# First batch's half loads in two 64-partition transfers of 1,024-byte runs, and unread products from a zeroed tile

## The chip, the cores and the metric

One core of a Trainium2 chip runs the kernel. TensorE (PE) multiplies matrices, VectorE (DVE), ScalarE (ACT) and GpSimd (POOL) work on tiles, and SyncE (SP) issues most of the DMA transfers. Each engine takes its instructions in the order of the program and waits on semaphores for the others. The metric is the device time of one execution in microseconds.

## The reference

Eight batches of causal attention with eight heads of 64 columns, 576 queries, and 592 keys (16 beacon keys that every query sees, then 576 causal ones); the result, as 4,608 rows of 512 columns, goes through a gated feed-forward layer.

```
k_all = np.concatenate([beacon_k, k], axis=2)
v_all = np.concatenate([beacon_v, v], axis=2)
scores = scale * np.matmul(q, k_all.transpose(0, 1, 3, 2))
scores = np.where(causal, -1000000000.0, scores)
a = softmax(scores)
x = (a @ v_all).transpose(0, 2, 1, 3).reshape(B * S, H * D)
out = (np.maximum(x @ w_gate, 0.0) * (x @ w_val)) @ w_out
```

Inputs and output are float32; the kernel multiplies in bfloat16.

## The kernel before

The whole work is cut into some 2,400 tasks. Each names its engine or engines, what it depends on and which tiles it holds, and a text constant `ORDER` in the source lists all of them in the order in which they are emitted, with the numbers of the buffers taken and, where a task may run on either of two engines, a letter (a ScalarE, v VectorE, g GpSimd). `replay` walks through this list, so each engine's program order is that of the list; a planner wrote it beforehand and is not part of the kernel. An entry such as `f12:7` stands for twelve unread products ("fills", line 1064): TensorE multiplies into bank 7, from which nobody reads, and so is kept at work while it would wait. Before the change a fill multiplies `ident` (a bf16 identity) with the zero part of `mask`. GpSimd makes both at the start (lines 436 to 444).

The first batch comes in halves. `load_half` (line 649 holds its transfer) loads 256 rows of four heads of q or k as a 128 x 512 float32 tile `st`, one transfer of 256 KB: each partition has two rows of each of four heads, so four runs of 512 bytes. There are eight such loads (k and q, two groups of four heads, two halves), all issued by SP. `rounded` (line 542) makes the bf16 tile `h`, on VectorE or GpSimd for this batch, and puts the columns of two heads side by side; `turned` (line 553) multiplies by `ident` to transpose it; an eviction (line 493 on ScalarE, 495 on VectorE) spreads the result into `kT` or `qT`. `load_rest` (line 677) does the same for the last 64 key rows with the 16 beacon rows, and for the first 64 and last 16 query rows, in runs of 256 bytes. Batches 1 and up load pairs of heads instead (line 587, runs of 1,024 bytes).

Scores (line 824) need halves and rest. For each block VectorE adds the mask and takes the minimum (line 772; q was negated), ScalarE takes the exponential with its sum (line 779), VectorE the reciprocal (line 785), GpSimd the product (line 790). For the first batch TensorE transposes the probabilities (line 900), for the others a DMA does (line 910, `pTb<-pb`, `pTa<-pa`). Line 920 and, for the last 16 queries of each head, 943 multiply by V. The feed-forward part (lines 981, 986 and 1012) runs over ten spans of 240 to 512 rows, each as soon as its rows are there; GpSimd issues the loads of the weights (line 507). Staging tiles `st` are eight buffers, taken in turn; a load waits until its buffer is free. Small memsets on VectorE zero the paddings of `qT` (469, 470), of `pa` and `pb` (463) and of the part of `xT` that holds the first batch's probabilities (485).

Of the kernel before, what the change touches and what calls it, by code (L numbers as in the profile page):

```python
# [10 lines left out]
BF16 = mybir.dt.bfloat16  # L11
# [66 lines left out]
10 1 22:0 2 26:1 34:3 0 4 30:2 23v:0.0 8 38:4 24:0 9 5 f4:7 42:5 27g:1.0 7 25v 48:7 28:1 46:6 35v:0 31v:2 36:3 29v 32:2 50:0 f3:7 37v 33a 54:1 f2:7  # L78
39v:1 410:4.5.0.0 58:2 11 431:6.0 6 40:1 411 43g:2 12 412 41a 423 44:2 413 45a 49g:0 422 3 436 414 448:3.1.0.0 62:7 415 421 f12:7 432 47g 426 68:5 450
416 459 70:6 449 425 460 51g:0 451 469:2.4 424 66:4 f1:7 417 437 461 14 52:5 427 433 55v:1 470 53a 418 56:6 434 f8:7 474 428 463 419 57v 471 429 462  # L80
420 59v:2 486:5.6.0.1 475 430 472 63v:0 454 473 438 487 64:2 453 435 60:7 464 69v 439 491 452 440:4 61a 72:0 476 495:3.1 13 73 441v:0 492 f3:7 455 465
496 488 444:0 467 f2:7 16 65v 504:4.5 497 77:1 489 500 442:2 445a:0 458 f3:7 505 457 f1:7 501 466 513:6.0 493 456 509 446:3 506 477 f1:7 f3:7 502 498
468 514 447a 443a 15 478:3 510 71v 482:4 518 522:1.2 515 19 511 524 479a:0 523:5.6 67g 516 519 483v:0 480:3 512 528 484:4 481a 18 525 548:7.3.2.3 485v
529 549 90:5 494 557:1.2 91 1734:4 553 17 550 1738:0 562 1735:0 566:5.6 507 503 1739:1 f2:7 558 563 1736:4 508 567 1742:7 559 490 1737:0 554 526 520
499 1740:4 571 1743:2 575:1.0 81:3 568 517 1741:1 82 1744:2 576 86:4 572 584:3.4 527 f1:7 580 1746:5 577 521 532:7 569 530 560 586 1747:1 531 536:1
533a:0 1748:5 1745:2 534:6 74:1.1 1749:3 537a 540:2 564 535v 587 78:2.1 95:0 544:5 542:1 541v:1 125:7 538:6 581 570 588 573 585:2.3 551 565 543a 555
539v 1750:0 561 545v 610:6.7.0 590 1751:1 552 546:4 589 578 611 591 1754:0 579 75:5 612 1752:1 1755:0 582 592 547v 76a 1756:3 574 613 1758:2 1757:5
593 594:4 1753:4 1759:0 596:5 556 595v:2 598:1 1762:0 583 614 79:7 597v 1760:4 1763:1 615 599a 602:2 1761:6 80a 606:5 87:1 616:1 604:4 617v:0 83:0
600:3 603v:3 92:2 101:3 84:6 601a 88:7 113:4 605v 607a 93:0 96:0 618:3 105:1 85a 89v 20 109:2 608:2 94a 99:6 97:5 126:1.0 609v 1766:1 98a 1764:4 619a
127:6 620:0.2.0.1 102:2 1765:7 128a 635:3.5 1770:7 1767:2 621 21 643 103:6 628 1768:4 622 1771:0 106:0 104a 1772:1 1769:8 624 1774:7 114:2 1773:9  # L90
1778:4 629 623 123:4 1776:1 1775:1 644 1779:2 1780:6 121:5 110:1 631 1792:4 1777:10 133:1 636 630 650:7.0 137:2 1781:11 1793:0 1787:2 637 129:0 645
646 659 107:6 652 639 111:4 1782:1 632 625 638 647 651 649 108a 112v 115:3 1788 633 653 640 116v 627 654 665:6.5 658 626 674:3.4 634 661 666 1794:7
642 660 670 1783 667 100:1 655 676 671 657 1784 119:6 124 677 700:0.6.2.3 1795:12 1785a:0 122 141:4 1796:5 701 679 117:3 668 656 708 715:7.1 702 678
648 1789 134:1 709 1797:1 704 669 717 145:1 1800:4 176:5 662 1790a:1 1798:3 716 664 723 703 1802:5 663 718 1799:13 641 1801:2 1804:2 724 1786 120 711
675:3.4 672 705 680 1803:14 149:6 1805:0 681 1806:0 726 683 682 1808:2 719 1807:15 673 690:3 1812:5 710 1809:1 712 130:0.0 730:6.0 684 725 1810:7 720
732 686 713 1814:1 738 1813:2 721 731 685 714 1816:5 1811:8 118 131:2 739 734 1818:4 687 1815:1 1817:1 689 745:3.7 733 1819:2 1820:1 688 741 735 746
754:5.6 132a 736 695:1 740 1822:4 750 722 1821:1 1824:0 757 142:0 747 1823:11 1828:1 151:7 707 751 756 755:3.4 138:2 1825:2 727 1832:2 742 748 758 737
# [12 lines left out]
913 961 1893:4 898 209a 220:2 973 211:2 960 1899:0 965 1894:1 955 964 962 1897:3 974 956:0 1896:1 1900:2 963 1901:6 1898:2 967 230:5 941:0 975 943:4  # L110
978 922 976 923 1903:1 977 214:7 944a 1902:3 227:1.0 942a 945:3 1904 966 979 221:1 980 986:5.3.4.6 225 1908:7 987 988 1913:0 215:0 998 991 981 968 201
1909 997 990 989 219 222:4 1910 999 242:1 992 256:6 957:5 1001 212:2 1911a:0 1905 213v 231:2.0 958a 1912 1000 216:5 970 238:2 1002 1906v:2 1914 234:7
993 217v 223 1007:3.4.6.7 946:1 995 250:4 1015 948:2 972 1918:5 949a 971 1016 252:3 985 1009 1915 1017 1907 947v 982 284:5 1008 983 1018 1105:1.2.1
268:0 228:6 1916a:1 1919 1106 1010 1917 1019 235:0 1107 1920 1011 229v 969 246:7 1108 1003 239:1 1923:3 1921v:0 1004 1109 1032:4.0.7.1.2.3 1110 1924:0
1925:2 1034 994 1111:1 996 1931:5 1033 1046 1038 1926:4 251:0 232:6 1927:3 1047 1932:2 264:4 1037 1012 1048 1013 1050 1929:2 1036 1051 1021 236:4 1035
1928:1 1933:5 233v 243:2 1039 1049 1040 1014 272:1 244:7 240:3 1930:5 247:0 237a 1022:0 1935:6 1053 245v 253:1 1112:4 1052 241v 1020 1936:0 1939:0
1934:6 1005 248:2 1113v 257:2 1059:1.5.3.7 249a 254:6 1940:1 1061 1943:4 255a 1070 260:6 1060 1937:2 1041 1944:2 1071 1043 1062 1947:6 1074 984 1054
1063 1938:3 1055 1941:0 1073 1006 1072 1064 1045 1945:2 1027:1 1065 273 1948:0 1949:1 1066 1044 1946:9 1075 269 1942:8 1080:3.4.5.6 1068 1025:2 1082
1058 1950:10 1023:0 1951:7 1026a 1057 1076 1042 1088 265:1 1955:1 1952:1 1081 1056 274:4 1957:2 1024v 1069 1922 1956:2 1089 1083 258:7 261:0 1953:0
1958:12 1090 1067 270:6 1078 1959:3 276:7 1091 1954:11 1079 1084 1092 262:1 259v 266:0 1093 1960:0 1114:5.4.2.6.0.1 286:3 263a 1028:7 275 1115 267a  # L120
1030:3 1128 1085 1077 1116 1029a 1961:1 1094 1031a 1129 1119 1087 1100:3 1967:7 1118 271 1132 1133 1962:13 1963:0 1120 1117 277:1.1 1130 1260:2.3.0
1131 1964:1 1965:5 1086 1968:0 1261 1135 278:1 1969:0 1966:14 1122 1095:2 1262 1971:7 1121 1263 1976:4 1134 1264 279v 1265 1141:5.3.6.2 1970:15 1977
1142 1123 1152 1972 1143 1266:0 1145 1144 1973 1146 1153 280:6 1147 1978 1974v:0 1155 1154 1981:3 1156 1975 1148 1979a:1 293:1 1162:0.1.5.6 1157 1980
# [199 lines left out]
def kernel(  # L323
# [12 lines left out]
    nc = tc.nc  # L336
# [181 lines left out]
    class Batch:  # L518
        pass

    batches = []

    def new_batch(b, prio, work):
        t = Batch()
# [573 lines left out]
```

## Time and profile before

| | us |
|---|---|
| median of two runs | 399.56 (399.12 to 400.01) |
| profiled execution, whole | 399.52 |
| its span on the core | 397.6 |

| engine | busy us | share of the span |
|---|---|---|
| PE | 380.1 | 96% |
| DVE | 274.2 | 69% |
| ACT | 270.3 | 68% |
| POOL | 231.0 | 58% |

A row of the timeline reads: start, duration, engine, line, operation, tile written and tile read, shapes, count, and in brackets the idle time before it with what ended it. SPq and ACTq are the queues in which these engines issue transfers. PEld is TensorE loading stationary tiles, beside its products. Matrix products are pipelined and their ends are modelled, so spacing says more than the duration of one.

### The profile page before, as it was taken

How to read it: one execution, taken by the hardware profiler on the slowest of the kernel's cores; microseconds unless marked ns; L12 is line 12 of the kernel's file. 1: busy time of each engine (PE TensorE's matmuls, PEld its weight loads, DVE VectorE, ACT ScalarE, POOL GpSimd, SP SyncE). 2: the span in 40 equal slices, each digit the busy share in tenths (PEclk: the TensorE clock that was granted, in tenths of full speed). 3: DMA queues.
4: the chain of work that ended last, by engine and by line, in shares of the span. 5: the costliest groups of instructions: out<-in, count | busy, mean ns of one | idle time of the engine just before them, and what ended most of it. 6: DMA issues, size and time to landing. Idle time of an engine off the chain costs nothing.

```text
span 397.6 us, 10026 instructions
## 1 busy us (share of the span) xinstructions
PE 380.1 (96%) x3384; PEld 199.7 (50%) x3428; DVE 274.2 (69%) x1008; ACT 270.3 (68%) x842; POOL 231.0 (58%) x447
## 2 busy tenths in 40 slices
PE   5789999999999999999999899999999999999996
PEld 3557855655454455454444454445444445444453
DVE  5899799888976888877876778567946832331230
ACT  1899699897877687789777789688746731332322
POOL 3799779959785789268827787663853650000000
PEclk9999999999999999999999999999999999999999
DMA  7999999999999999968997999988897556001102
GB/s 183 218 181 237 193 230 235 195 230 236 215 234 205 313 177 203 181 186 177 202 205 215 197 202 198 209 162 167 169 180 161 101 105 168 28 0 54 54 26 94
DMA packets 184100, 68.89 MB, mean 173 GB/s; under 512 B 158384, under 2 KB 179504, under 8 KB 184048
## 3 DMA queue, kind: packets, MB, share of 16 engines
q1 hardware_dynamic: 179216, 63.46, 74.5%
q0 software_dynamic: 4752, 4.72, 7.3%
q8 instruction: 27, 0.44, 0.5%
q14 instruction: 25, 0.20, 0.1%
q10 hardware_dynamic: 80, 0.07, 0.1%
HBM read 38.54 MB, written 9.44 MB: 121 GB/s over the span
## 4 chain that ended last, share of the span: by engine, by line
PE 83%; DMA 3%; issue 1%; DVE 1%; POOL 0%; ACT 0%; DVEq 0%
PE f L1012 22%; PE f L986 22%; PE f L981 22%; PE f L824 6%; PE f L920 6%; PE f L553 2%; DMA pTb<-pb 2%; DMA pTa<-pa 2%; PE f L943 1%; PE f L626 1%; PE f L874 1%; DVE f L772 0%; PE f L900 0%; POOL pa L790 0%; DVE kT L495 0%
## 5 line engine op out<-in xcount | busy, mean ns | idle before, releaser
L790 POOL TENSOR_SCALAR pb<-pb,small 128x384 bf16<-128x384 bf16 (+8 forms) x272 | 142.1, 538 | 45.5 <-DVE small L785 43.9
L779 ACT ACTIVATE pb<-f,small 128x448 bf16<-128x448 f32 (+8 forms) x272 | 144.8, 551 | 24.5 <-DVE small L772 19.7
L772 DVE CUSTOM_DVE_ANT_0 f<-f,mask 128x64 f32<-128x64 f32 (+8 forms) x288 | 136.3, 507 | 20.1 <-PE f L824 11.0
L997 DVE TENSOR_TENSOR hT<-g,f 128x512 bf16<-128x512 f32 (+3 forms) x120 | 74.4, 629 | 55.3 <-PE f L986 30.2
L981 PE MATMUL f<-xT,wg_r 128*128 128x512 bf16 (+3 forms) x466 | 108.1, 357 | 0.9 <-issue 0.2
L986 PE MATMUL f<-xT,wv_r 128*128 128x512 bf16 (+3 forms) x465 | 106.8, 357 | 1.2 <-issue 0.3
L1012 PE MATMUL f<-wo_r,hT 128*128 128x512 bf16 (+3 forms) x441 | 100.3, 374 | 1.5 <-issue 1.0
L992 ACT ACTIVATE g<-f 128x512 f32<-128x512 f32 (+3 forms) x120 | 65.8, 563 | 49.3 <-PE f L981 31.0
L981 PEld LDWEIGHTS <-wg_r 128*128 128x128 bf16 x480 | 45.0, 98 | 45.2 <-issue 2.5
L986 PEld LDWEIGHTS <-wv_r 128*128 128x128 bf16 x480 | 44.5, 98 | 44.2 <-issue 3.0
L1012 PEld LDWEIGHTS <-hT 128*128 128x128 bf16 (+3 forms) x456 | 41.9, 100 | 47.0 <-issue 2.9
L779 ACT ACTIVATION_READ_ACCUMULATOR pb<-f,small 128x1 f32 x272 | 60.0, 221 | 0.0
L542 POOL TENSOR_SCALAR h<-st 128x512 bf16<-128x512 f32 (+1 forms) x87 | 46.8, 547 | 22.5 <-DMA st<-in_q_dram 5.0
L772 DVE DVE_READ_ACCUMULATOR2_ANT small<- 128x1 f32 x296 | 41.2, 139 | 0.1
L824 PE MATMUL f<-kT,qT 64*64 64x64 bf16 (+7 forms) x640 | 34.6, 296 | 1.6 <-ACT pb L779 0.7
L497 POOL TENSOR_SCALAR v<-st 128x512 bf16<-128x512 f32 (+1 forms) x38 | 23.3, 616 | 19.7 <-DMA st<-in_v_dram 19.6
L493 ACT CAST xT<-f 128x240 bf16<-128x240 f32 (+2 forms) x46 | 16.1, 376 | 22.6 <-PE f L920 22.5
L785 DVE RECIPROCAL small<-small 128x2 f32<-128x2 f32 (+3 forms) x136 | 19.7, 160 | 12.0 <-ACT pb L779 10.8
L920 PE MATMUL f<-pTb,v 128*64 128x320 bf16 (+3 forms) x488 | 27.0, 254 | 0.4 <-DMA pTb<-pb 0.4
L824 PEld LDWEIGHTS <-qT 64*64 64x64 bf16 x640 | 14.7, 107 | 22.6 <-issue 17.7
L920 PEld LDWEIGHTS <-v 128*64 128x64 bf16 (+1 forms) x512 | 21.0, 109 | 9.9 <-issue 5.1
L553 PE MATMUL f<-ident,h 128*128 128x128 bf16 (+1 forms) x224 | 19.8, 222 | 5.7 <-DVE h L542 5.0
(62 smaller groups left out, 216.1 us busy)
## 6 DMA issues: line engine op xcount, KB each, us to landing
out_dram<-osb SPq DMA_DIRECT2D x34, 256.0 KB, 2.7
st<-in_k_dram SPq DMA_DIRECT2D x28, 256.0 KB, 4.6
st<-in_q_dram SPq DMA_DIRECT2D x28, 256.0 KB, 4.0
st<-in_v_dram SPq DMA_DIRECT2D x24, 256.0 KB, 4.6
st<-in_q_dram SPq DMA_DIRECT2D x16, 128.0 KB, 3.8
st<-in_k_dram SPq DMA_DIRECT2D x16, 128.0 KB, 4.1
st<-in_v_dram SPq DMA_DIRECT2D x8, 224.0 KB, 4.5
wv_r<-in_moe_w_val_dram POOLq DMA_DIRECT2D x3, 512.0 KB, 9.2
```

The costliest lines, as they stand in the source:

```text
L542: (nc.gpsimd if x.engine == "POOL" else nc.vector).tensor_scalar(to, src, by, 1.0, ALU.mult, ALU.mult)
L553: nc.tensor.matmul(to, h16.tile[:rows, a * P:(a + 1) * P], ident[:rows, :rows], start=True, stop=True)
L772: nc.vector.tensor_tensor_reduce(out=view(i, n - m), in0=view(i, n - m), in1=msk, scale=1.0, scalar=at(7) if m < n else 3.0e38, op0=ALU.ad ...
L779: nc.scalar.activation(ph.tile.rearrange("p a n -> p (a n)")[:, a:a + n], view(i), AF.Exp, bias=at(i), scale=-1.0, accum_out=at(4 + i))
L790: nc.gpsimd.tensor_scalar(one, one, at(8 + i), 1.0, ALU.mult, ALU.mult)
L824: nc.tensor.matmul(banks[k][b_].tile[64 * i:64 * i + 64, off:off + n], t.q.tile[r, 2 * g + i, 64 * j:64 * j + 64], t.kT.tile[r, 2 * g + i, ...
L920: nc.tensor.matmul(ps.tile[64 * hh:64 * hh + 64, d0:d0 + w], t.v.tile[:rows, c, D * h:D * h + D], rhs(64 * hh), start=(c == 0), stop=(c == ...
L981: nc.tensor.matmul(psg.tile[:, :mt], wg_r[:, ki, nf * P:(nf + 1) * P], xT[:, ki, m0:m0 + mt], start=(ki == 0), stop=(ki == KM - 1))
L986: nc.tensor.matmul(psv.tile[:, :mt], wv_r[:, ki, nf * P:(nf + 1) * P], xT[:, ki, m0:m0 + mt], start=(ki == 0), stop=(ki == KM - 1))
L992: r = add("ACT", c_act(mt), lambda _, psg=psg, g=g: nc.scalar.activation(g.tile[:, :mt], psg.tile[:, :mt], AF.Relu), (a,), (psg, g), -1000 ...
L997: hid.append(add("DVE", c_dve(mt), lambda _, psv=psv, g=g, nf=nf: nc.vector.tensor_mul(hT[nf].tile[:, :mt], g.tile[:, :mt], psv.tile[:, :m ...
L1012: nc.tensor.matmul(ps[c].tile[64 * c:64 * c + rows, :w], hT[nf].tile[:, t0:t0 + rows], wo_r[:, nf, w * c:w * c + w], start=(nf == 0), stop ...
```

## The change

- `load_half` issues two transfers for each load. Transfer i fills partitions 64 i to 64 i + 63 with the heads 4 g + i and 4 g + i + 2; each partition has four rows of two heads, so two runs of 1,024 bytes. The rounding depends on both. The shapes of rounding and eviction stay, their strides follow the new layout.
- Either transfer can go through SP's or ScalarE's queue. The order gives ScalarE the second halves of the first four loads, ahead of its table load; both halves of the last four loads are issued by SP, one after the other.
- A new tile `idle` is zeroed by VectorE, as its first instruction. The fills multiply it with itself, and no longer read `ident` and `mask`.
- `ORDER` is written anew, for the whole kernel, with nine tasks more. It has 53 fills and not 46; fourteen of them stand before the first transposition. GpSimd makes the causal helper of the last queries first, then `ident`, then `mask`. The first `qT` eviction goes to ScalarE.

```
+    idle = cp.tile([P, 256], BF16, name="idle")
...
+    def make_idle(_):
+        nc.vector.memset(idle, 0.0)
...
-            def fetch(_):
-                nc.sync.dma_start(st.tile.rearrange("p (h e) -> p h e", h=4),
-                                  src[b, 4 * g:4 * g + 4, s0:s0 + 256, :].rearrange("h (p j) d -> p h (j d)", j=2))
-
-            ld = add("DMA", (0.5, 0.95), fetch, (held,), (st,), prio[0])
+            st.users += 1
+
+            def fetch(i):
+                def run(x):
+                    (nc.scalar if x.engine == "ACT" else nc.sync).dma_start(
+                        st.tile[64 * i:64 * i + 64].rearrange("p (k e) -> p k e", k=2),
+                        src[b, bass.ds(4 * g + i, 2, step=2), s0:s0 + 256, :].rearrange("k (p j) d -> p k (j d)", j=4))
+
+                return run
+
+            ld = add("DMA", (0.7, 0.4), fetch(0), (held,), (st,), prio[0])
...
-                to.rearrange("p (x k d) -> p k x d", k=2, x=4), src.rearrange("p (k x d) -> p k x d", k=2, x=4))])
+                to.rearrange("p (j k d) -> p k j d", k=2, j=4), src.rearrange("p (k j d) -> p k j d", k=2, j=4))])
+            second.append((fetch(1), st, ca))
...
-                copy(x.engine, dst.tile[:, 2 * g:2 * g + 2, c0:c0 + 256].rearrange("p i (n j) -> p i n j", j=2),
-                     ps.tile.rearrange("p (i j n) -> p i n j", i=2, j=2))
+                copy(x.engine, dst.tile[:, 2 * g:2 * g + 2, c0:c0 + 256].rearrange("p i (n j) -> p i n j", j=4),
+                     ps.tile.rearrange("p (j i n) -> p i n j", i=2, j=4))
...
-            nc.tensor.matmul(to[:, :256], ident, mask.bitcast(BF16)[:, :256], start=True, stop=True)
-
+            nc.tensor.matmul(to[:, :256], idle[:, :P], idle, start=True, stop=True)
+
+    for run, st, ca in second:
+        x = add("DMA", (0.7, 0.4), run, (), (st,))
+        x.users.append(ca)
+        ca.deps.append(x)
+        ca.left += 1
+    on_idle = add("DVE", 0.2, make_idle)
```

The first entries of the two orders (22, 26, 34, 30, 38 and 42 are SP's first loads; 2399 to 2402 the transfers on ScalarE; 2407 the new memset):

```
-10 1 22:0 2 26:1 34:3 0 4 30:2 23v:0.0 8 38:4 24:0 9 5 f4:7 42:5 27g:1.0 7 25v 48:7 28:1 46:6 35v:0 31v:2
+2407 11 4 22:0 2399a 3 2 26:1 2400a 34:3 0 5 1 30:2 f4:7 23v:0.0 9 38:4 2401a 8 12 f10:7 24:0 42:5 2402a 27g:1.0 f2:7
```

More of the change, by code (lines that the diff above doesn't have):

```diff
@@ L82 @@
[L82 to L97, printed above, removed]
@@ new lines @@
+1736:4 508 567 1739:1 f2:7 559 1742:7 503 1737:0 568 498 571 494 1740:4 575:1.0 1743:2 499 516 1741:1 563 1746:5 576 517 584:3.4 572 1744:2 569 512
+530 520 580 577 532:7 521 560 1747:0 1745:2 536:1 533a:0 531 586 1748:5 534:6 78:2.1 1749:3 537a 540:2 535v 587 544:5 570 542:1 541v:1 538:6 581
+74:1.1 588 551 585:2.3 578 543a 539v 552 95:0 1750:0 545v 589 125:7 610:6.7.0 590 1751:1 546:4 579 611 591 1754:0 561 109:2 555 1752:1 564 612 1755:0
+547v 565 75:5 613 1756:3 592 573 1753:4 556 594:4 76a 614 1762:0 593 582 1757:5 595a:2 596:5 583 598:1 1758:2 597v 574 1760:4 1759:0 79:7 599a 83:0
@@ new lines @@
+642 665:6.5 674:3.4 655 660 649 666 1783 661 100:1 670 667 1784 627 119:6 677 671 662 145:1 633 676 1794:7 663 129:0 1785a:0 700:0.6.2.3 122 668
+1795:12 1796:5 678 648 708 702 124 1789 137:2 1797:1 679 701 1786 669 709 715:7.1 703 141:4 1798:3 704 134:1 724 176:5 1800:4 710 120 717 1790a:1
+1802:5 657 716 1801:2 680 1799:13 1804:2 149:6 718 681 711 1803:14 675:3.4 656 723 1806:0 1805:0 672 682 683 725 1808:2 673 719 690:3 712 1807:15
+1812:5 726 714 684 730:6.0 1809:1 118 1810:7 1813:2 738 685 664 731 1816:5 1811:8 130:0.0 686 1814:1 732 1817:1 1818:4 720 687 734 1815:1 688 745:3.7
@@ new lines @@
+1914 958v 1003 216:5 1912 1005 1007:3.4.6.7 217v 234:7 946:1 948:2 1015 947a 221 1915 949a 223 1016 1009 1105:1.2.1 250:4 1017 993 1918:5 1008 994
+1018 995 256:6 1106 1919 1010 231:2.0 252:2 981 1019 1107 1011 1920 1916v:1 970 1108 985 1917 228:6 1923:3 235:0 1109 1921v:0 1032:4.0.7.1.2.3 1110
+246:7 229v 1924:0 1922 1931:5 239:1 1033 1111:1 1034 996 232:6 1925:2 1036 1038 243:2 1046 268:0 1927:3 1037 251:0 1926:4 1932:2 272:1 972 1035 236:4
+284:5 1933:5 1012 1928:1 1047 1013 233a 1048 240:3 237a 969 1935:6 1934:6 1014 1050 1051 247:0 1022:3 241v 1929:2 1040 984 1049 253:1 244:7 1039
@@ new lines @@
+1930:5 1112:4 1936:0 269 1939:0 1052 1113v 257:2 245v 1053 248:2 982 254:6 1940:1 1054 983 1059:1.5.3.7 1041 249a 1943:4 1020 1071 255a 1060 1058
+260:6 1937:2 1070 1944:2 264:4 1006 1061 276:7 1941:0 1062 1004 1063 273 1064 1938:3 1947:6 1073 1021 1942:8 1074 1056 1027:1 1945:2 1948:0 1072 1045
+1065 1949:1 1055 1946:2 1075 1080:3.4.5.6 265:1 1950:10 1025:2 1043 1081 1023:0 1955:1 1026a 261:0 1082 1044 1024v 1951:7 1083 1088 1907 1956:2 1957:2
+270:6 1066 1089 1952:1 274:3 1953:0 1091 286:4 1958:12 1090 1076 258:7 1079 262:1 1954:11 1084 1959:3 1092 1078 259v 266:0 1094 1114:5.4.2.6.0.1
@@ new lines @@
+1182:1 1211 2006:12 2008:0 2011:7 1228 2010:4 1220 1178:6 1235:0.1.4.5 2012:2 1179v 295:2.3 1244 2013:7 297a 1243 296a 2015:6 1221 1231 1246 2014:5
+1232 326:3 1245 2019:2 1222 1237 1212 2016:0 1236 1198 2017:3 1990 303:0 1238 316:0 2021:7 2018:6 1197 1239 299 1247 2023:5 2020:1 1240 1224 309:2
+2022:13 314:7 1269:0.2.3.4.0.1 1241 2024:2 1980 1180:1 1270 1234 1286 1183:7 1185:5 1181a 1271 308:1 2025:6 1213 1186v 1275 1284 1199 2027:1 1184a
+1223 1274 2026:8 1242 2031:7 1272 1233 1283 1250:0 1273 1287 1249 304:5.6 1288 1285 1248 2029:0 1289 305v 2028:0 310:2 306v 2033:3 2032:1 323:0.0
@@ new lines @@
+1690 2216:2 1674 2221:6 1680 1678 1685 1691 405 2223:5 2218:9 1684 1683 2225:2 1694 1686 2222:10 1689 1693 2227:3 1692 2224:0 1688 1729 1700:6.7.0.1
+2226:11 1695 1730 1645:5 1701 2228:0 1687 1731:1 1648:2 1650:4 1702 2229:3 1649v 1703 1696 1709 1697 2231:2 1704 1708 1699 1646a 2235:6 1663 1705
+2230:12 1711 1676 1710 1651v 2237:7 1706 2232:0 1712 1732:5 2236:1 1662 2233:1 1665 2238:14 1707 2239:3 1698 2234:13 1715:1 1675 1733v 2241:7 1713
+2240:2 1714 2258:4 1677 2243:3 2259 1720:3 2253:1 2248:2 2244 2242:15 2254 2249 2255 2260 2256a:0 2245 2257 1721:5 1716:6 1718:0 1722v 1717v 1723:7
@@ L171 @@
+2318 2348:1 2344:0 2345:3 2323 2346:5 2350:0 2355:4 2324a:1 2353:0 2356:0 2352:2 2357:2 2354:1 2363:5 2359:3 2364:2 2367:7 2360:1 2319a:2 2365:0 2320
+2361:3 2325 2366:4 2371:4 2362:3 2369:0 2358:2 2372:1 2368:0 2373:2 2375:1 2374:10 2377:4 2370:8 2376:2 2379:6 2378:11 2384:0 2380 2381 2385 2382a:0
+2383 2386 2389:5 2387a:1 2390 2388 2391 2394:4.6 2392v:2 2393 2397:1 2395v:0 2398 2396
 """
@@ L519 @@
         pass
-    batches = []
+    batches, second = [], []
     def new_batch(b, prio, work):
```

137 lines of the change are left out of this document (63 added, 74 removed), and 6 rows, old and new, of the table ORDER.

## The prediction

> **What bounds the kernel now.** I read the page first, then the chain of waits, then a table of windows, then the ramp in the timeline.
>
> ```profile
> span 397.6 us, 10026 instructions
> ...
> PE 83%; DMA 3%; issue 1%; DVE 1%; POOL 0%; ACT 0%; DVEq 0%
> ```
>
> The profiled execution took 399.52 us: the span and 1.92 us around it. The median shown is 399.56 us, so a sum made on the profiled run can be held against it as it is. TensorE carries 83% of the chain that ended last. The table by windows says where it does not (time span, length, busy time and count of PE, PEld, DVE, ACT, POOL, then granted clock, DMA share, GB/s):
>
> ```profile
> 0.00:4.37 4.37, 0.00 (x0) 0.00 (x0) 0.84 (x11) 1.28 (x1) 2.68 (x13) 1.00 0.48 138
> 4.37:15.00 10.63, 9.48 (x78) 5.46 (x79) 9.11 (x63) 4.67 (x20) 4.42 (x8) 1.00 0.97 233
> 15.00:33.00 18.00, 15.15 (x176) 10.29 (x173) 17.73 (x70) 17.48 (x61) 16.80 (x34) 1.00 1.16 193
> 33.00:394.00 361.00, 355.45 (x3139) 183.99 (x3180) 246.11 (x867) 246.56 (x761) 207.09 (x393) 1.00 0.81 172
> ...
> 0.00:33.00 33.00, 9.16 (x46) 4.98 (x46) 1.00 1.01 198
> ```
>
> The last row counts line 1064 alone, the unread products ("fills"): all 46 lie before 33 us. From 33 us to 394 us TensorE idles 361.00 - 355.45 = 5.55 us, so there the kernel is its own matrix work. Before 33 us it is a ramp: TensorE waits and fills, while VectorE (17.73 of 18) and ScalarE (17.48 of 18) are full from 15 us on. The matrix work itself does not change, so the change is worth what it takes off the ramp, plus or minus what the new order of the rest costs in idle time. The ramp has these VectorE waits and rows:
>
> ```profile
> DVE h L542 <- DMA st<-in_k_dram: 2.6, 1, 2.6
> DVE f L772 <- PE f L824: 0.8, 1, 0.8
> ...
> 0.81 1.28 ACT L493 ACT_TABLE_LOAD   x1 [0.81 <-PEq L1082]
> 0.81 0.47 SPq L649 DMA_DIRECT2D st<-in_k_dram  x1
> 0.88 0.25 DVE L463 MEMSET pb<- 128x32 uint32 x5 [0.88 <-PEq L1082]
> 3.89 0.43 DVE L542 TENSOR_SCALAR h<-st 128x512 bf16<-128x512 f32 x1 [2.64 <-DMA st<-in_k_dram]
> 3.94 0.62 SPq L677 DMA_DIRECT2D st<-in_beacon_k_dram  x1
> 4.37 0.61 PE L553 MATMUL f<-ident,h 128*128 128x128 bf16 x4 [4.37 <-DVE h L542]
> 5.13 0.65 DVE L495 CAST kT<-f 128x512 bf16<-128x512 f32 x1
> 6.79 0.49 DVE L542 TENSOR_SCALAR h<-st 80x256 bf16<-80x256 f32 x2 [0.17 <-DMA st<-in_beacon_k_dram]
> 7.20 1.31 DVE L495 CAST qT<-f 128x512 bf16<-128x512 f32 x4
> 7.69 0.49 ACT L493 CAST kT<-f 128x256 bf16<-128x256 f32 x2 [5.60 <-PE f L553]
> 8.65 0.75 PE L824 MATMUL f<-kT,qT 64*64 64x64 bf16 x16
> 9.35 0.23 DVE L772 CUSTOM_DVE_ANT_0 f<-f,mask 128x64 f32<-128x64 f32 x1
> 9.60 0.31 DVE L485 MEMSET xT<- 128x128 uint32 x2
> 10.97 0.09 DVE L469 MEMSET qT<- 128x32 uint32 x1
> 11.01 0.11 DVE L470 MEMSET qT<- 128x64 uint32 x1
> 12.06 2.74 PE L1064 MATMUL f<-mask,ident 128*128 128x256 bf16 x12
> 14.97 0.28 PE L1064 MATMUL f<-mask,ident 128*128 128x256 bf16 x1
> 15.09 0.43 DVE L772 CUSTOM_DVE_ANT_0 f<-f,mask 128x256 f32<-128x256 f32 x1 [0.80 <-PE f L824]
> 15.54 1.04 PE L1064 MATMUL f<-mask,ident 128*128 128x256 bf16 x8
> ```
>
> VectorE waits 2.64 us for the first data, then works nearly without a gap to 14.29 us, where it stands 0.80 us for scores that queue on TensorE behind twelve fills.
>
> **The change part by part.** *First scores: nothing.* They wait for the rest rows of K, whose last piece (beacon_k, the sixth transfer on SP) is issued at 3.94 us and taken at 6.79 us. That place on SP is kept: SP still issues two halves, then the four rest pieces. In the new order VectorE evicts the first kT tile (0.65 us) after this and no longer before, and leaves the first qT tile (about as long) to ScalarE. Before: 1.31 us of evictions after the rest; after: 0.65 + (1.31 - 0.65) = 1.31 us. Two queues can bring the first tile sooner, but its wait of 2.64 us sits in front of another that ends later, so I take 0; at most it is SP's 0.47 us if halves are issued in no time, and below nothing if ScalarE's next two halves delay the rest rows: 256 KB at the rate below, 0.75 us.
>
> *ScalarE issues four transfers* ahead of its table load. By SP's 0.47 us each: 1.9 + 1.28 us from 0.81 us, free at 4.0 us. Its first work came at 7.69 us, and the qT tile that it takes over was evicted from 7.20 us on: 3 us of cover. Without it the cost would be the 1.9 us.
>
> *Runs of 1,024 bytes.* The first row is a stretch of 512-byte packets (0.41 MB in 813), the second one of about 970 bytes (0.37 MB in 382):
>
> ```profile
> 2.60:3.80 1.20, 0.00 (x0) 0.00 (x0) 0.00 (x0) 0.00 (x0) 0.93 (x4) 1.00 1.13 340
> 45.30:46.30 1.00, 1.00 (x17) 0.84 (x14) 0.47 (x2) 0.55 (x2) 0.96 (x3) 1.00 1.07 375
> ```
>
> A 256 KB load takes 0.77 us at 340 GB/s and 0.70 at 375: 0.07 us, 0.6 us for all eight, spread over transfers that nobody waits for longer than the 0.3 us of the rest rows. I take 0, bounds 0 and 0.6 us of gain.
>
> *SP issues twice as often for the last four loads:* 4 x 0.47 = 1.9 us more, with V loads behind them:
>
> ```profile
> 12.20 2.63 SPq L725 DMA_DIRECT2D st<-in_v_dram  x3
> 35.17 0.71 PE L920 MATMUL f<-pTb,v 128*64 128x320 bf16 x10
> ```
>
> Those V rows are multiplied from 35.17 us on: hidden. Whether the loads themselves come late is rival C.
>
> *Memsets.* The new program zeroes the second qT (0.09 + 0.11 us) and the xT padding (0.31 us) before the first minimum; in the old one they stand between minima. That takes 0.51 us out of a full VectorE. The new memset of the unread tile, about as large as the padding of one qT (0.1 us), lies in the 2.64 us wait. The rounding and evictions have the same shapes with other strides: nothing.
>
> *Fills.* 53 in place of 46: fourteen stand ahead of TensorE's first useful product, and seven, not twelve, ahead of the scores for which VectorE stood still. In the timeline the twelve cost (2.74 - 0.28) / 11 = 0.224 us each and the eight just after (1.04 - 0.28) / 7 = 0.109 us, although the granted clock reads 1.00 throughout: TensorE runs at half its later speed until about 14.9 us. Seven fills at 0.224 us cost 1.57 us, 1.17 us less than 2.74. VectorE, now 0.51 us ahead, would need 0.80 + 0.51 = 1.31 us less to feel no stall; 0.14 us of it stays. So VectorE reaches this point 1.17 us earlier. The fourteen in front can start when VectorE, free at 0.88 us, has zeroed their tile, say at 1.2 us, and end at 1.2 + 14 x 0.224 = 4.3 us; the first real product starts at 4.37 us, so they cost nothing.
>
> *The new order of everything else.* By the two orders written in the code, of 214 tasks with a choice of engine 31 move from ScalarE to VectorE and 23 the other way; from 33 us on both are busy 68% (246 of 361), so that is nothing. How well the new order packs TensorE is not in this trace. The nearest row is the 5.55 us of idle time after 33 us, with this as its longest wait:
>
> ```profile
> PE f L943 <- DMA pTa<-pa: 1.4, 1, 1.4
> ```
>
> I take 0, bounds one such wait more or one fewer.
>
> Sum: 399.52 - 1.17 = 398.35 us. VectorE and ScalarE are full from there to 33 us, so I let the whole lead reach the saturated part.
>
> **The rivals.**
>
> *A: forecast,* 398.4 us, own range 397.7 to 399.2.
>
> *B: the lead is lost.* VectorE gets to 33 us earlier, but the re-made order leaves a wait that the old one had not. One wait like 1.4 us gives 399.52 - 1.17 + 1.4 = 399.8 us. For it: the order differs everywhere; against it: the old one has a single such wait in 361 us.
>
> *C: slower, through half transfers on SP.* The last four loads become eight 64-partition transfers on SP alone. The first and the last of the four:
>
> ```profile
> 8.35 0.91 SPq L649 DMA_DIRECT2D st<-in_k_dram  x1
> ...
> 11.78 0.37 SPq L649 DMA_DIRECT2D st<-in_q_dram  x1
> 17.06 0.43 DVE L542 TENSOR_SCALAR h<-st 128x512 bf16<-128x512 f32 x1
> ...
> DMA to landing us min/median/max: 3.1/4.2/4.7
> ```
>
> Should a transfer into half the partitions run at half the rate, each load takes 1.54 us and not 0.77, 3.1 us more for four, in a stretch where the DMA share is already 0.97 to 1.16. The last one, issued at 11.78 us, lands near 16.0 and is taken at 17.06 us: the first 1.1 us are free, and beyond that VectorE stands still, 2.0 us. That gives 398.35 + 2.0 = 400.4 us. No row shows such a transfer alone, so the factor is open between 1 and 2, and it decides from 1.35 on. [...]
>
> *D: TensorE speeds up earlier.* Fourteen fills back to back from 1.2 us might bring the 0.109 us spacing from about 4.5 us on. Then the seven fills take 0.76 us and the rest of the stall, 0.14 us, goes; the first scores (0.75 us at 8.65 us) halve, 0.4 us sooner: 398.35 - 0.14 - 0.4 = 397.8 us. Against it: from 4.37 us on the old kernel kept TensorE 89% busy (9.48 of 10.63 us) and it kept the 0.224 us spacing until the end of that. [...]
>
> *The change doesn't do what it says:* should ScalarE's transfers start only after its table load, the first tile comes 1.3 us later, still before the rest rows; that falls to A.
>
> **How the numbers follow.** A 0.42, B 0.22, C 0.20, D 0.10; another 0.06 lies beyond all of these, mostly from the new order. The likeliest is A: 398.4 us. The low end is A with one wait of 1.4 us fewer, 397.0, which takes in D and D with the DMA gain (397.2); the high end is C with one more issue of 0.47 us on SP ahead of its last half, 400.9. A measurement of this kernel can tell 2% (8 us) from no change; nothing above reaches that. It would take six waits of 1.4 us, or the gain of nearly half the time before 15 us plus all fills. Faster 0.01, within 0.96, slower 0.03.
>
> **What would show it.** Right: VectorE's wait near 14 us down to 0.1 to 0.2 us; the first minimum still near 9.3 us; fills from about 1.2 us; TensorE's idle time after 33 us between 4 and 7 us. C shows as VectorE or GpSimd waiting on st from q or k between 12 and 18 us. D shows as fill spacing of 0.11 us before 9 us. The forecast is wrong if first data land later than 3.9 us and the first scores with them, or if the new order's idle time after 33 us differs by over 1.5 us: then the ramp was not what decided.

## The result and the profile after

| | before | after |
|---|---|---|
| median, us (two runs each) | 399.56 (399.12 to 400.01) | 406.12 (405.62 to 406.61) |
| ratio to before, 95% interval | | 1.0146 [1.011, 1.0182] |
| profiled execution, its span | 399.52, 397.6 | 406.61, 404.5 |

The change costs 6.6 us, 1.5%; forecast were 398.4 us and a range of 397.0 to 400.9. By the bound of 2% this is "no change", but with an interval that excludes 1. The profile page after the change, span and chain of waits:

```profile
span 404.5 us, 10087 instructions
...
PE 78%; DMA 12%; ACT 3%; DVE 2%; POOL 2%; issue 1%; SPq 0%; ACTq 0%; POOLq 0%; DVEq 0%
```

DMA holds 12% of the chain; it held 3%. The windows say where the time lies (columns as before: span of time, length, busy time and count of PE, PEld, DVE, ACT, POOL, then granted clock, DMA share, GB/s; rows with a single pair have PE alone):

```profile
4.37:15.00 10.63, 8.17 (x72) 4.61 (x73) 7.22 (x53) 5.14 (x21) 4.06 (x7) 1.00 0.90 214
15.00:33.00 18.00, 13.51 (x119) 7.83 (x118) 13.43 (x55) 13.28 (x45) 12.23 (x26) 0.81 1.10 180
...
20.00:21.00 1.00, 0.00 (x0) 1.00 1.35 261
24.00:30.00 6.00, 5.33 (x42) 0.50 1.16 177
...
33.00:400.79 367.79, 364.20 (x3236) 1.00 0.80 170
```

From 15 to 33 us VectorE was busy 17.73 us and ScalarE 17.48; now 13.43 and 13.28. The granted clock, 1.00 in every window shown of before, reads 0.50 from 24 to 30 us. Behind 33 us TensorE idles 367.79 - 364.20 = 3.59 us; the 5.55 us of before can't be set beside that, for a reason given with the new order below. What VectorE waited for in the ramp (total, times, longest, in us):

```profile
DVE h L546 <- DMA st<-in_q_dram: 3.4, 1, 3.4
DVE h L546 <- PE f L557: 2.3, 1, 2.3
DVE f L783 <- PE f L835: 1.8, 4, 0.8
DVE h L546 <- DMA st<-in_k_dram: 1.3, 1, 1.3
```

The second of these, put down to TensorE, ends at 7.69 us with the q rest rows; in run 5, the same kernel, it is put down to their transfer.

The timeline of the ramp, cut to the first batch's transfers and those who take them (L546 rounds what L656 and L688 load; L783 is the minimum, L992 the first feed-forward product, L1023 the last):

```profile
0.80 0.72 ACTq L656 DMA_DIRECT2D st<-in_k_dram  x1
0.81 0.74 SPq L656 DMA_DIRECT2D st<-in_k_dram  x1
1.60 0.84 SPq L656 DMA_DIRECT2D st<-in_q_dram  x1
2.86 0.63 ACTq L656 DMA_DIRECT2D st<-in_q_dram  x1
4.29 0.43 DVE L546 TENSOR_SCALAR h<-st 128x512 bf16<-128x512 f32 x1 [1.29 <-DMA st<-in_k_dram]
4.49 0.61 SPq L688 DMA_DIRECT2D st<-in_beacon_k_dram  x1
8.49 0.49 DVE L546 TENSOR_SCALAR h<-st 80x256 bf16<-80x256 f32 x2 [0.27 <-DMA st<-in_beacon_k_dram]
10.94 0.23 DVE L783 CUSTOM_DVE_ANT_0 f<-f,mask 128x64 f32<-128x64 f32 x1
12.91 1.68 PE L1075 MATMUL f<-idle 128*128 128x256 bf16 x7
13.34 1.24 SPq L656 DMA_DIRECT2D st<-in_q_dram  x2
13.55 0.93 POOL L511 DMA_DIRECT2D wv_r<-in_moe_w_val_dram  x1
14.99 0.43 DVE L783 CUSTOM_DVE_ANT_0 f<-f,mask 128x256 f32<-128x256 f32 x1 [0.78 <-PE f L835]
21.46 0.43 DVE L546 TENSOR_SCALAR h<-st 128x512 bf16<-128x512 f32 x1 [3.42 <-DMA st<-in_q_dram]
33.06 0.58 PE L992 MATMUL f<-xT,wg_r 128*128 128x240 bf16 x4
391.42 9.37 PE L1023 MATMUL f<-wo_r,hT 128*128 128x512 bf16 x60
```

Before, the two marks at the end stood here:

```profile
27.55 0.99 PE L981 MATMUL f<-xT,wg_r 128*128 128x240 bf16 x8
384.51 9.36 PE L1012 MATMUL f<-wo_r,hT 128*128 128x512 bf16 x59
```

Two steps make the ramp late. The rest rows of K are taken at 8.49 us and not 6.79, and with them the first minimum falls at 10.94 us, not 9.35: 1.6 us. Then the last q half is taken only at 21.46 us, after a wait of 3.42 us, and TensorE, which gets its next operand from there, stands for 2.49 us. The row of that line for the last two halves alone, with the time from issue to landing:

```profile
L656 SPq DMA_DIRECT2D st<-in_q_dram x2: 595/600/605, 13.3 to 14.0; - x2
...
DMA to landing us min/median/max: 2.8/5.1/7.4
```

An issue takes 0.60 us; a pair with the wait between stands as 1.25 us. The first half of the pair lands in 2.8 us. The second, issued at 14.0 us, 0.4 us after GpSimd's weight load of 512 KB (13.55 us), takes 7.4. The first feed-forward product starts 33.06 - 27.55 = 5.5 us later than before, the last block of products 391.42 - 384.51 = 6.9.

### The profile page after: what moved, and what is told of

Same layout as the page of the kernel before. It is cut to its first block, busy times and chain, and to the rows that moved or that the text cites. A ratio compares the mean times of both kernels' runs of the same rounds, so it can differ in the third digit from the quotient of the medians.

```text
span 404.5 us, 10087 instructions
## 1 busy us (share of the span) xinstructions
PE 389.0 (96%) x3435; PEld 202.4 (50%) x3435; DVE 281.0 (69%) x1014; ACT 270.6 (67%) x837; POOL 231.5 (57%) x447
## 4 chain that ended last, share of the span: by engine, by line
PE 78%; DMA 12%; ACT 3%; DVE 2%; POOL 2%; issue 1%; SPq 0%; ACTq 0%; POOLq 0%; DVEq 0%
PE f L992 21%; PE f L1023 21%; PE f L997 20%; PE f L931 5%; PE f L835 5%; DMA pTb<-pb 4%; DMA st<-in_k_dram 3%; DMA st<-in_q_dram 3%; DMA wo_r<-in_moe_w_out_dram 2%; PE f L557 2%; ACT pb L790 2%; PE f L911 1%; POOL pb L801 1%; PE f L954 1%; PE f L630 1%
## 5 line engine op out<-in xcount | busy, mean ns | idle before, releaser
L801 POOL TENSOR_SCALAR pb<-pb,small 128x512 bf16<-128x512 bf16 (+8 forms) x272 | 143.0, 547 | 69.1 <-DVE small L796 54.3
L783 DVE CUSTOM_DVE_ANT_0 f<-f,mask 128x192 f32<-128x192 f32 (+8 forms) x288 | 136.8, 508 | 21.3 <-PE f L835 11.4
L992 PE MATMUL f<-xT,wg_r 128*128 128x512 bf16 (+3 forms) x480 | 108.7, 358 | 0.0
L1023 PE MATMUL f<-wo_r,hT 128*128 128x512 bf16 (+3 forms) x456 | 102.7, 374 | 1.1 <-DMA wo_r<-in_moe_w_out_dram 1.0
L992 PEld LDWEIGHTS <-wg_r 128*128 128x128 bf16 x480 | 44.6, 98 | 45.3 <-issue 3.7
L1023 PEld LDWEIGHTS <-hT 128*128 128x128 bf16 (+3 forms) x456 | 41.9, 100 | 47.8 <-issue 3.9
L546 POOL TENSOR_SCALAR h<-st 128x512 bf16<-128x512 f32 (+1 forms) x87 | 47.3, 553 | 19.9 <-DMA st<-in_q_dram 5.4
L790 ACT ACTIVATION_READ_ACCUMULATOR pb<-f,small 128x1 f32 x272 | 58.7, 216 | 0.0
L783 DVE DVE_READ_ACCUMULATOR2_ANT small<- 128x1 f32 x296 | 41.5, 140 | 0.1
L497 ACT CAST xT<-f 128x320 bf16<-128x320 f32 (+2 forms) x39 | 14.8, 387 | 16.2 <-PE f L931 15.9
```

Of the source, the lines that this page charges most:

```text
L546: (nc.gpsimd if x.engine == "POOL" else nc.vector).tensor_scalar(to, src, by, 1.0, ALU.mult, ALU.mult)
L783: nc.vector.tensor_tensor_reduce(out=view(i, n - m), in0=view(i, n - m), in1=msk, scale=1.0, scalar=at(7) if m < n else 3.0e38, op0=ALU.ad ...
L790: nc.scalar.activation(ph.tile.rearrange("p a n -> p (a n)")[:, a:a + n], view(i), AF.Exp, bias=at(i), scale=-1.0, accum_out=at(4 + i))
L801: nc.gpsimd.tensor_scalar(one, one, at(8 + i), 1.0, ALU.mult, ALU.mult)
L992: nc.tensor.matmul(psg.tile[:, :mt], wg_r[:, ki, nf * P:(nf + 1) * P], xT[:, ki, m0:m0 + mt], start=(ki == 0), stop=(ki == KM - 1))
L1023: nc.tensor.matmul(ps[c].tile[64 * c:64 * c + rows, :w], hT[nf].tile[:, t0:t0 + rows], wo_r[:, nf, w * c:w * c + w], start=(nf == 0), stop ...
```

## The experiments

Each ratio is to the kernel before, run beside it on the same chip (its median was 399.8, 400.2, 400.5 and 400.1 us in the four sets).

**1. All eight loads as one transfer, new order and fills kept.**

```
-22:0 2399a 3 2 26:1 2400a 34:3 0
+22:0 3 2 26:1 34:3 0
...
+                nc.sync.dma_start(st.tile.rearrange("p (h e) -> p h e", h=4),
+                                  src[b, 4 * g:4 * g + 4, s0:s0 + 256, :].rearrange("h (p j) d -> p h (j d)", j=2))
```

> The changed kernel with all eight half loads as one 128-partition transfer from SP again; its order and its zeroed fills stay. Theory T (the half transfers make the loads late, above all the last of them, taken at 21.46 us against 17.06): about 399.5 us, between 398.5 and 401, and VectorE's 3.4 us wait for q is gone. Theory R (the newly written order of the whole kernel is what costs): still 404 to 406 us. Theory F (the zeroed fills): still about 406 us.

400.93 us (399.86 to 402.33), ratio 1.004 [1.0014, 1.0066], as theory T has it, and VectorE's wait of 3.4 us is gone. The split is most of the loss. The timeline of this kernel (L848 scores, L1088 fills), for what remains:

```profile
1.13 3.17 PE L1088 MATMUL f<-idle 128*128 128x256 bf16 x14 [1.13 <-DVE idle L442]
7.81 0.36 PE L848 MATMUL f<-kT,qT 64*64 64x64 bf16 x12 [0.40 <-DVE qT L499]
8.86 0.23 DVE L796 CUSTOM_DVE_ANT_0 f<-f,mask 128x64 f32<-128x64 f32 x1
11.12 1.68 PE L1088 MATMUL f<-idle 128*128 128x256 bf16 x7
27.57 0.58 PE L1005 MATMUL f<-xT,wg_r 128*128 128x240 bf16 x4
```

And a window of it (PE alone, then granted clock):

```profile
9.00:19.00 10.00, 8.55 (x68) 0.50 1.26 239
```

The first minimum is 0.5 us sooner than before, as the moved memsets and earlier scores let one expect, and yet the first feed-forward product stands at 27.57 us, where it was (27.55). The twelve score products take 0.36 us (0.030 each; before 0.75 for 16, 0.047), so TensorE had its pace early; then the granted clock falls to 0.50 from 8.9 to 19.1 us, and the seven fills cost 0.24 us each.

**2. The last four loads as one transfer** (the same edit where `half` is 1), the first four split over SP and ScalarE.

```
+            if half:
+                nc.sync.dma_start(st.tile.rearrange("p (h e) -> p h e", h=4),
```

> The changed kernel with only the last four half loads as one transfer each; the first four stay split over SP and ScalarE. T with its seat in the last four loads: 400 to 401.5 us, the first scores still near 9.9 us, no wait over 1 us for the last q. T with its seat in the first four: 404 us or more. R: 404 to 406 us.

402.99 us (401.76 to 404.27), 1.008 [1.0055, 1.0105]. Timeline of this kernel:

```profile
8.57 0.49 DVE L546 TENSOR_SCALAR h<-st 80x256 bf16<-80x256 f32 x2 [0.26 <-DMA st<-in_beacon_k_dram]
11.03 0.23 DVE L796 CUSTOM_DVE_ANT_0 f<-f,mask 128x64 f32<-128x64 f32 x1
```

The first minimum is as late as in the changed kernel, and VectorE has no long wait for the last q half. Neither reading had this time: both parts of the split have a share. Splitting the first four costs 402.99 - 400.93 = 2.1 us; the first minimum is 2.2 us later than in run 1, and the first feed-forward product starts at 29.45 us, between run 1's 27.57 and the changed kernel's 33.06.

**3. The order and fills of before, all eight loads split,** ScalarE and SP as in the change.

```
-22:0 2 26:1 34:3
+22:0 2399a 2 26:1 2400a 34:3
```

> The kernel before, with its own order and its own fills, and only the loads split as in the change (four second halves from ScalarE, four from SP right behind the first). T: 404 to 407 us. R: within 1 us of 399.6. F: within 1 us of 399.6.

402.7 us (401.71 to 403.97), 1.0075 [1.005, 1.01]. The split costs 2.9 us in the old order too, less than theory T's least. The first minimum is at 10.93 us; the last half was issued at 13.0 us, ahead of the weight load (13.55), landed in 3.9 us, and nobody waited for it.

**4. Before, with fills from a zeroed tile alone.**

```
-            nc.tensor.matmul(to[:, :256], ident, mask.bitcast(BF16)[:, :256], start=True, stop=True)
+            nc.tensor.matmul(to[:, :256], idle[:, :P], idle, start=True, stop=True)
```

> The kernel before, with only the operand of its 46 fills changed to the zeroed tile, memset first on VectorE; places and number of the fills stay. T and R: 399.6 us within 0.6. F: 402 us or more, with fills that no longer speed TensorE up near 15 us.

400.41 us (398.59 to 402.68), 1.0018 [0.9984, 1.0052]: nothing that can be told from 0.

**5. The changed kernel again,** on the chip of runs 6 to 8.

> The changed kernel as it is, beside the others on one chip: 405 to 407 us by every theory; the place to compare from.

408.05 us (406.91 to 409.69), 1.0179 [1.0118, 1.024]. This is above the 405 to 407 expected. The weight load was issued at 13.66 us, the last half at 14.2; it was taken at 22.10 us, 7.9 us after its issue and after a wait of 3.96 us: the wait is there again.

**6. GpSimd's first weight load moved behind two of its later products.**

```
-426 417 470 437 450 14 52:5
+426 417 470 437 450 52:5
...
-65v 495:3.1 13 444:0
+65v 495:3.1 14 13 444:0
```

> The changed kernel; GpSimd issues its first weight load two products of line 801 later, near 17 us and not at 13.55 us. Theory W (the very last half transfer, issued at 13.99 us, takes 7.4 us to land because the 512 KB weight load got ahead of it by 0.4 us): it lands within 5 us, VectorE's wait of 3.4 us for q is gone, and the time is 402 to 404 us. Rival H (a transfer into 64 partitions is slow in itself, or the V loads behind it take its bandwidth): the wait stays over 2 us and the time at 405 or more.

404.32 us (403.0 to 405.29), 1.0084 [1.0058, 1.0111]: 3.7 us less than run 5, a little over theory W's range. Timeline of this kernel:

```profile
13.77 1.25 SPq L656 DMA_DIRECT2D st<-in_q_dram  x2
17.15 0.93 POOL L511 DMA_DIRECT2D wv_r<-in_moe_w_val_dram  x1
18.96 0.47 DVE L546 TENSOR_SCALAR h<-st 128x512 bf16<-128x512 f32 x1 [0.50 <-DMA st<-in_q_dram]
```

The last pair is issued later than in the changed kernel, and taken 2.5 us sooner; its second half, issued at some 14.4 us (13.77 + 1.25 - 0.60), is taken 4.5 us later, with the same V loads behind it. The first feed-forward product starts at 29.90 us (32.37 in run 5). What made the half late was the weight load ahead of it, not the pair itself.

**7. Only the first k and the first q load split,** the other six in one transfer.

```
+            if (g or half):
+                nc.sync.dma_start(st.tile.rearrange("p (h e) -> p h e", h=4),
```

> The changed kernel with only the loads of k and q of the first group and first half split over SP and ScalarE, all other six in one transfer. Theory I (SP's longer issues of the two split loads, 0.74 and 0.84 us for 0.47 and 0.50, and their packets delay the rest rows): first minimum at 10.2 us or later, 402.5 to 403.5 us. Theory X (ScalarE's two further halves, which nobody needs yet, go ahead of the rest rows on the DMA engines): first minimum by 9.6 us, 401 to 402 us.

402.52 us (400.88 to 404.51), 1.0049 [1.0014, 1.0084]; first minimum at 9.60 us, between runs 1 and 2. ScalarE's two further halves therefore make up 1.4 of the 2.2 us by which the first minimum moved. The first minimum is theory X's, the time theory I's: SP's longer issues and the halves of the first two loads, which stay together here, keep the other 0.7 us.

**8. Before, with the two q rest transfers of the first batch issued by ScalarE.**

```
-                    nc.sync.dma_start(s3[at:at + n], heads(src, b, s0, n))
+                    (nc.scalar if b == 0 and kind == "q" else nc.sync).dma_start(s3[at:at + n], heads(src, b, s0, n))
```

> The kernel before with nothing changed but the queue of the first batch's two q rest transfers: ScalarE and not SP, full 128-partition loads throughout. If the place of the rest rows in SP's queue sets the first scores: first minimum at 8.0 to 8.7 us for 9.35, and 398.5 to 399.4 us. If a lead in the ramp is lost again before 33 us, as one transfer per load in the new order showed (0.5 us earlier, first feed-forward product at the same time): 399.8 us within 0.5.

400.06 us (397.19 to 402.72), 0.9991 [0.9956, 1.0027]. SP issued the rest of K 1.3 to 1.4 us sooner, and it was still taken at 7.20 us, after 6.79 before; the first minimum, 10.11 us, was later, which neither reading had. An earlier issue alone brought no earlier rows in this stretch, where the DMA engines had a busy share of 1.07 (first 15 us of this run).

**9. The changed kernel with twelve more fills** ahead of the transposition that waited for the last half.

```
-439 462 472 487 64:2
+439 462 472 487 f12:7 64:2
```

> The changed kernel with twelve more unread products on TensorE ahead of the transposition of the last q half, where TensorE stood still from 19.5 to 22.0 us and the granted clock fell to 0.50 until 30 us. Theory K (part of the 3.7 us that the late last half cost is the clock behind the gap): the clock stays up from 22 us on, the first feed-forward product comes 1 to 2 us earlier than 32.4 to 33.1 us, time about 406.5 us beside 408 for the changed kernel. Rival N (VectorE, not TensorE, sets the ramp behind the gap): the clock stays up or comes back sooner, but the first feed-forward product stays near 32.4 to 33.1 us and the time at 408. Rival F (twelve at 0.23 us are not enough to keep the clock): clock 0.50 behind the gap as before, 408.

407.69 us (406.29 to 408.49), 1.0177 [1.0137, 1.0218]: no gain, and none of the three in clean form. In its profiled execution (the fastest of its four) GpSimd's weight load went out at 14.43 us and the last half at 13.95, so the long wait did not arise; the first feed-forward product came at 29.82 us. TensorE's waits behind the ramp show that this was lost again:

```profile
PE f L557 <- POOL h L546: 2.1, 1, 2.1
PE f L931 <- DMA pTb<-pb: 2.1, 2, 1.5
```

Two of its windows, the second from 33 us to TensorE's last product:

```profile
119.00:120.00 1.00, 1.00 (x7) 0.50 1.28 291
...
33.00:400.55 367.55, 362.65 (x3206) 1.00 0.79 169
```

Work left at 33 us fell from 364.20 to 362.65 us, but idle time behind it rose from 3.59 to 4.90, and a gap of 2.1 us at 117 us was followed by three microseconds at half clock.

**10. The order and fills of before, only the last four loads split,** all halves from SP.

```
-50:0
+50:0 2403
...
-62:7
+62:7 2406
```

> The kernel before, its order and fills, with only the last four of the first batch's loads split in two, all eight halves from SP; the first four stay one transfer. Theory S (a pair costs SP 1.25 us and not 0.45, and what is lost is where the last half stands against GpSimd's weight load): first minimum near 9.4 us as before; the last q half issued near 14 us; if that falls behind the weight load (issued 13.2 to 13.7 us) VectorE stands over 2 us for it and the time is 402.5 to 404; if it falls ahead, the wait is under 0.5 us and the time 400 to 401. Rival T (the two parts add up whatever their order: 2.9 us for all eight in this order, less the 2.1 us that the first four cost in the new one): 400.7 us with a small wait. Rival H (a half transfer runs at half the rate): landing above 5 us for all of the last eight.

401.06 us (399.24 to 403.11), 1.001 [0.9975, 1.0044]. Timeline of this kernel:

```profile
12.53 1.25 SPq L664 DMA_DIRECT2D st<-in_q_dram  x2
14.01 1.05 POOL L507 DMA_DIRECT2D wv_r<-in_moe_w_val_dram  x1
```

From the answer for the line of the split loads:

```profile
DMA to landing us min/median/max: 3.1/3.5/5.0
```

And the window from 33 us to the last product:

```profile
33.00:393.48 360.48, 358.99 (x3187) 1.00 0.82 172
```

Eight halves on SP, ahead of the weight load, cost nothing that can be told from 0; the interval leaves room for 1.8 us, so rival T's 0.8 us is not excluded. They land in 3.1 to 5.0 us; whole loads took 3.1 to 4.7. The profiled execution is the fastest of the ten.

**11. Before, with zeroed fills and fourteen more of them in front.**

```
-10 1 22:0
+2399 f14:7 10 1 22:0
```

> The kernel before with fills from a zeroed tile, and fourteen more fills ahead of TensorE's first useful product; loads and order otherwise as before. Theory D (a busy TensorE from 1.1 us on runs at its full pace before 9 us): fill spacing 0.11 us before 9 us, first scores 0.3 to 0.4 us sooner, stall at 14 us gone, 398.5 to 399.5 us beside 400.0. Theory A (the pace comes as late as before): spacing 0.22 us to 14 us, 400.0 to 400.6, not to be told from the kernel before. A later first scores than 9.4 us would say that the fourteen cost the ramp something.

400.07 us (398.74 to 405.4), 0.9988 [0.9965, 1.0011]: no gain. The pace did rise early, as theory D has it: the sixteen score products take 0.47 us and not 0.75, and start 0.4 us sooner. But the first minimum, at 9.29 us, is where it was (9.35), and the twelve fills near 12 us still take 2.74 us:

```profile
8.24 0.47 PE L828 MATMUL f<-kT,qT 64*64 64x64 bf16 x16
11.44 2.74 PE L1068 MATMUL f<-idle 128*128 128x256 bf16 x12
```

The window there shows that the pace had been taken back:

```profile
12.00:14.00 2.00, 2.00 (x11) 0.50 1.18 291
```

**12. Before, with seven fills and not twelve** ahead of the scores for which VectorE stood still.

```
-421 f12:7 432
+421 f7:7 432
```

> The kernel before with seven unread products and not twelve ahead of the scores for which VectorE stood still 0.80 us near 15 us; nothing else. The prediction's term (twelve at 0.224 us are 2.74 us, seven 1.57, so the stall of 0.80 goes, and all of it reaches the part where TensorE is full): stall under 0.1 us, first feed-forward product 0.8 us earlier, 0.8 us less time, ratio 0.998. Theory L (a lead of under 1 us at 15 us is taken back by the transfers and weights that the next steps wait for, since all of them stay where they were): stall gone or smaller, first feed-forward product within 0.3 us of before, ratio 1.000. Rival K2 (TensorE, less at work, gets its full pace later): 0.22 us spacing behind 15 us, later first feed-forward product, ratio 1.002 or more.

401.32 us (397.56 to 403.27), 1.002 [0.999, 1.005]. In the profiled execution, the fastest of twelve:

```profile
11.34 0.94 PE L1064 MATMUL f<-mask,ident 128*128 128x256 bf16 x7
26.35 0.89 PE L981 MATMUL f<-xT,wg_r 128*128 128x240 bf16 x7
```

The stall is gone, the first feed-forward product comes 1.2 us sooner and the span is 395.6 us. That is 2.0 us less than before's profiled execution, which lies near its median; the fastest of the 17 executions of before beside this run took 398.5 us, 0.9 more than this one's 397.6. So a lead can reach the end, as far as one execution shows. But here the seven took 0.13 us each and not 0.224, so 0.6 us of it is a pace that rose sooner. Four of the twelve executions had a mean granted clock of 0.994 to 0.996 and took 402.3 to 403.3 us; the eight at 0.998 and above took 397.6 to 401.7. The middle does not move.

## Why the prediction was wrong

Two steps that were put at nothing failed: "SP issues twice as often for the last four loads", called hidden, and "First scores: nothing". In their place the last half fell behind GpSimd's weight load, and the first minimum came 1.6 us late. By the medians: order and fills +1.1 us (run 1 against before), the first four loads +2.1 (run 2 against run 1), the last four +3.4 to +4.6 (the changed kernel's +6.6, and +7.8 in run 5, less run 2's +3.2). Of run 5's 7.8 us the weight load's place makes 3.7 (run 6), the pairs without it 0.9 (run 6's +4.1 less run 2's +3.2, not to be told from 0). The profiles give a second cut, from single executions, against run 10 with its order of before: 364.20 - 358.99 = 5.2 us more work left at 33 us, and 3.59 - 1.49 = 2.1 us more idle time behind it; together the 7.3 us between their last products. One of the prediction's own signs came true: the first data were taken at 4.29 us, later than 3.9, and the first scores came late with them.

- **First scores.** Taken at 0, with bounds of -0.47 and +0.75 us; they came 1.6 us late, in run 2 as well. The 0.75 was the right mechanism (ScalarE's next two halves ahead of the rest rows), and run 7 shows that leaving those two whole takes back most of it. Its size was too small: those two halves made 1.4 us. Missing were SP's issues: the first two took 0.74 and 0.84 us and not 0.47, so the last rest piece was issued at 4.49 and not 3.94 us. Run 8 warns against taking issue time for the whole cause.
- **SP's double issue,** the larger of the two. Priced at 4 x 0.47 us, hidden by cover. A 64-partition half takes 0.60 us to issue; a pair keeps SP 1.25 us where one load took 0.37 to 0.51 for most. The V rows were indeed covered. What the pairs moved was the last half, from 11.78 to 14.0 us, behind GpSimd's weight load at 13.55.
- **Rival C** named the place, the last halves on SP, and not the mechanism. A half on SP lands about when a whole load does (2.8 to 5.0 us; whole loads 3.1 to 4.7 before, 3.0 to 5.5 in run 1), except the one behind the weight load (7.4). As it has half the bytes, that does not settle its rate; it says that the half itself cost no time here. The half rate from which C's 2.0 us come was the author's supposition, and no run shows it. With the first loads' halves in flight from two queues the DMA engines moved as much as before (345 GB/s for 340):

```profile
2.70:3.30 0.60, 0.60 (x5) 0.42 (x4) 0.30 (x1) 0.00 (x0) 0.51 (x2) 1.00 1.01 345
```

  Run 6 takes the weight load away from it and 3.7 us of time with it; run 10 has the pairs without it, at no cost that can be told from 0. So where C had 2.0 us the runs show about nothing, or over 3 us, as two queues fall within half a microsecond. For the first four loads one transfer was 2.1 us faster than two to disjoint partition halves (run 1 against run 2), though run 7 puts most of their delay down to which transfers went ahead; for the last four in the old order there is no difference that can be told from 0 (run 10).
- **ScalarE's issues and its table load** were hidden as said, though an issue took it 0.62 to 0.72 us and not 0.47: its table was loaded by 4.80 us, its first eviction ran at 7.59.
- **Fills and memsets, -1.17 us.** The stall of 0.78 us stayed (predicted 0.14), as TensorE came later along with VectorE. Where the loads were right, in run 1, the lead of 0.5 us at the first minimum was lost by 27.57 us; in one execution of run 12 such a lead reached the end; in its median it did not.
- **D, an earlier pace.** In the changed kernel the seven fills take 0.24 us each at 12.91 us: not so. In runs 1 and 11 the pace did rise early and was taken back, in run 1 until 19.1 us, past the 14.9 us of before; neither run gained by it. That the pace would rise at about 4.5 us was the author's estimate; in run 11 the fourteen fills in front took 0.23 us each (3.17 us) and the four at 4.69 us 0.15 (0.60 us).
- **The new order (B).** The old order's wait for `pTa` (1.4 us) is gone, and new ones stand in its place: TensorE waits 1.4 us for a half rounded by GpSimd (2.1 in run 9, and 1.8 in run 1, with whole loads) and 1.0 us for output weights. 2.1 us more idle time in all, more than the one wait that B counted.
- **The 5.55 us of idle time** behind 33 us, from which the prediction took its sign of 4 to 7 us, are too many. The profile of before lacks 44 product records, as its page shows beside run 10's, which has the same order:

```profile
PE 380.1 (96%) x3384; PEld 199.7 (50%) x3428; DVE 274.2 (69%) x1008; ACT 270.3 (68%) x842; POOL 231.0 (58%) x447
...
PE 383.5 (96%) x3428; PEld 200.1 (50%) x3428; DVE 274.4 (69%) x1008; ACT 270.1 (68%) x842; POOL 231.3 (58%) x447
```

  All 44 are products of 512 columns in the feed-forward part, and a missing product counts as idle time. With all its records run 10 idles 1.49 us; so the changed kernel's 3.59 us, of which no record is missing either, are more and not fewer.

Open: how the 3.7 us of run 6 divide between the wait itself, the half clock behind it, and the order after it. Run 9 was meant to tell, but there the weight load went out 0.9 us later as well. Why the new order costs 1.1 us in run 1 is read from its waits and was not tested alone.

## What to carry to other kernels

A transfer split in two cost the issuing queue twice or more here (1.25 us for a pair, some 0.5 for one load), and what that does must be read at the place to which it pushes the last one: ask which other queue's large transfer it now falls behind. Transfers added early in this ramp delayed those that the first result needs, even from an idle queue (first minimum at 9.60 us in run 7, at 11.03 in run 2 with two more halves from ScalarE). Time gained early is not yet time gained at the end: run 1's lead of 0.5 us was gone by the first feed-forward product, behind a stretch at a granted clock of 0.50, though no run shows that the clock alone took it. And before idle time of one profile is compared with that of another, see that both have all their products: in the kernels here PE and PEld count the same when they do (3,428 and 3,428 in run 10, 3,435 and 3,435 after the change, 3,384 and 3,428 before).

## What the runs showed of the hardware

- A transfer issued 0.4 us behind a 512 KB weight load from GpSimd's queue took 7.4 us to land; its twin, issued 0.65 us sooner, 2.8 us. In run 5 the late half was taken 7.9 us after its issue; with the weight load out of the way, in run 6, 4.5 us after.
- An issue from SP took 0.60 us for 64 partitions with two runs of 1,024 bytes, and 0.37 to 0.51 us mostly for 128 partitions with four of 512; while ScalarE issued too, 0.74 and 0.84. In run 8 the first two whole loads took 0.47 and 0.50 us beside ScalarE's issues.
- The granted clock fell and rose again within a run (0.50 from 24 to 30 us in the changed kernel, 1.00 from 33 us on). It fell to 0.50 after 2.5 us without products in the changed kernel and after 2.1 us in run 9 (at 117 us), and in run 1 with no gap above 0.5 us but TensorE only 54 to 60% busy from 7 to 9 us. A reading of 1.00 early in a trace is not the full pace: fourteen fills at 1.12 us in the changed kernel took 0.23 us each with it (3.17 us), eight at 15.54 us in the kernel before 0.13 (1.04 us), at 1.00 too.
- Of the 92 timed runs of the kernel before, 8 had a mean granted clock under 0.9975, and their median was 402.4 us; for the others it was 400.0.
